# Building the stage-2 sine tables on all 128 lanes, loading K weights earlier and holding back the Wo copies

## The chip, the cores and the metric

The kernel runs on one core of one Trainium2 chip. The metric is microseconds (us) of device time for one execution. Executions of the kernel before alone spread from 2157.94 to 2175.35 us within one call of eleven runs, that is 0.8%. So a few us of change are hard to see in whole times, and much of this study reads *marks* in the traces: the moment at which a certain instruction ends or a certain store is issued.

## The reference

Two independent parts share the core, and their outputs stand side by side.

```python
def _A_ref(q, k, v, shift_k, ssm_k, ssm_D):       # S = 2048, D = 1024
    # k_shift: a causal convolution of k with 4 taps
    kv = k_shift * v
    # a long causal convolution by FFT of length 2 * S, per channel
    y = irfft(rfft(kv_padded) * rfft(ssm_k_padded))[:S]
    return q * (y + kv * ssm_D)

def _B_ref(x, mem0, Wq, Wk, Wv, Wo, seg_len):     # 32 heads of 128, 64 segments of 32
    mem = mem0
    for s in range(n_seg):
        h = concat([mem, x_segment])              # 8 memory rows and 32 new ones
        # q, k, v = h Wq, h Wk, h Wv; masked softmax attention; o = (...) Wo
        mem = o[:, :8]
        outs.append(o[:, 8:])
```

The kernel does part A's FFT by matrix products in a front of about 440 us. In the same time it computes the K and Q projections of all x for part B (those need no memory). Then come 64 segments, one after the other, which stream weights from DRAM.

## The kernel before

The front first makes the tables Mre, Mim, Nre, Nim of the second FFT stage by sines. VectorE computes integer phases, and ScalarE evaluates the sine of one lane block after another, because each block of lanes goes to other columns of the table:

```python
def act_sin(out_ap, a_int_ap, nbits, p0=0):
    nc.scalar.activation(out_ap, a_int_ap, ACT.Sin, bias=pi_col[p0:...], scale=...)
...
for x, (M, n) in enumerate(((Mre, nxr), (Mim, nxi))):
    aM = phases(x)...                              # VectorE: phases
    for (r0, c0) in [(0, 0), (64, 32)]:
        act_sin(M[r0:r0 + 64, :, c0:c0 + 32], aM[r0:r0 + 64], 12, r0)
for y, (N, ph) in enumerate(((Nre, (1024, 0)), (Nim, (2048, 1024)))):
    ...
    for (r0, c0) in [(0, 0), (32, 64), (64, 0), (96, 64)]:
        act_sin(N[r0:r0 + 32, :, c0:c0 + 64], aN[r0:r0 + 32], 12, r0)
```

Then stage 1 runs over 16 rows. A few words first: a lane is one of the 128 rows of a tile; an eviction is the copy of a finished matmul result (`s_ps`) to a tile from which it can be stored (`s_sb`); a chunk is a piece of weights of 512 KB; a unit is one step of stage 2. A row has two halves: the k half (transposes, a copy to `kt`, four matmuls, two evictions by ScalarE, one store to SK) and the u half (eight products on VectorE, four matmuls, two evictions by ScalarE, one store to SU):

```python
for t in range(16):
    # 8 transposes of ssm_k on the tensor engine
    nc.scalar.copy(kt[:], pt[:])
    stage1(kt, t, SK1)             # matmuls, 2 ScalarE evictions s_sb, store
    ...                            # loads of k and v, every second row
    # uacc and prod: 7 VectorE products and sums
    nc.vector.tensor_tensor(out=u[:], in0=acc[:], in1=Vt, op=ALU.mult)
    su_stores.append(stage1(u, t, SU1))
stage1_done(su_stores)
```

`stage1_done` belongs to part B. It loads x rows, transposes them to XBT (copied by ScalarE), loads eight K-weight chunks `pw`, each held until the store of a certain row has been issued, and runs the first K projection, 128 matmuls into `kb_ps`:

```python
make_xbt(su)                       # x loads held to su[X_LOAD + tb]
for kc in range(8):
    with tc.issue_after(su[K_LOAD + kc].ins):
        group(0, 0, which=[kc], ws=ws)
for _ in dense(0, 0, ws): pass     # kb_ps
```

Stage 2 of the FFT follows in units of `pa`, `pb` products. Between units `fill()` does some of part B's work. Every third unit it transposes one block of x; a load `X_sb` fetches two blocks at a time and is asked for when both blocks before it are done. It also issues the copies of Wo chunks from DRAM to the ring buffer in DRAM:

```python
if n >= WO_COPY and wo_copies:
    nc.gpsimd.dma_start(dst_view(stream_src(ch), ch), dram_chunk(ch))
if n % 3 == 2 and blocks:
    b = blocks.pop(0)
    x_block(b)
    if b % 2 and blocks:
        x_load(b + 1)
```

A scheduler decides the final order of the instructions on each engine, its queue.

Of the kernel before, what the change touches and what calls it, by code (L numbers as in the profile page):

```python
# [24 lines left out]
INLINE = {1: 0, 3: 1, 5: 0, 11: 1, 12: 0, 14: 1}  # L25
N2, N3 = 12, 15
WO_COPY = 27
X_LOAD, K_LOAD = 3, 7
RING = 6

PITCH = 2048


def a_kernel(ctx: ExitStack, tc, q, k, v, shift_k, ssm_k, ssm_D, outa, slot16, stage1_done, fill):
    nc = tc.nc
    S, D = 2048, 1024
    NP = 34
    NS = 17
# [10 lines left out]
    Mre = const.tile([128, NP, 64], BF, name="Mre")  # L49
    Mim = const.tile([128, NP, 64], BF, name="Mim")  # L50
    Nre = const.tile([128, NS, 128], BF, name="Nre")
    Nim = const.tile([128, NS, 128], BF, name="Nim")
# [4 lines left out]
    with ExitStack() as c1:  # L57
# [15 lines left out]
        def phases(x):  # L73
            return ints[:, 1088 * (x + 1):1088 * (x + 2)]
# [33 lines left out]
        def act_sin(out_ap, a_int_ap, nbits, p0=0):  # L108
            nc.scalar.activation(out_ap, a_int_ap, ACT.Sin, bias=pi_col[p0:p0 + out_ap.shape[0], 0:1],
                                 scale=-2.0 * PI / (1 << nbits))  # L110
# [57 lines left out]
        for hf in range(4):  # L168
            pt = ps_big.tile([128, 1024], F32, tag="big", name="sh_ps")
            for e in range(2):  # L170
# [18 lines left out]
        nxr = cw.tile([128, 1], F32, name="nxr")  # L189
        nc.vector.tensor_tensor(out=nxr[:], in0=nx[:], in1=phr[:], op=ALU.add)  # L190
        nxi = cw.tile([128, 1], F32, name="nxi")
# [5 lines left out]
        nc.vector.tensor_scalar(out=w_f[:], in0=w_i[:], scalar1=kp[:, 0:1], scalar2=None, op0=ALU.add)  # L197
        nc.vector.tensor_tensor(out=aN0, in0=w_f[:].unsqueeze(2).to_broadcast([128, NS, 32]),
                                in1=kn2[:].unsqueeze(1).to_broadcast([128, NS, 32]), op=ALU.mult)
        for x, (M, n) in enumerate(((Mre, nxr), (Mim, nxi))):  # L200
            aM = phases(x).rearrange("p (a b) -> p a b", b=32)
            nc.vector.tensor_scalar(out=aM, in0=v_i, scalar1=p_n2[:, 0:1], scalar2=n[:, 0:1], op0=ALU.mult, op1=ALU.add)
            nc.vector.tensor_scalar(out=aM, in0=aM, scalar1=4095, scalar2=None, op0=ALU.bitwise_and)
            for (r0, c0) in [(0, 0), (64, 32)]:
                act_sin(M[r0:r0 + 64, :, c0:c0 + 32], aM[r0:r0 + 64], 12, r0)
            nc.gpsimd.memset(M[32:64, 0, :], 0.0)
        for y, (N, ph) in enumerate(((Nre, (1024, 0)), (Nim, (2048, 1024)))):
            aN = phases(y).rearrange("p (a b) -> p a b", b=64)
            for x in range(2):
                nc.vector.tensor_scalar(out=aN[:, :, 32 * x:32 * x + 32], in0=aN0, scalar1=ph[x], scalar2=None, op0=ALU.add)  # L210
            nc.vector.tensor_scalar(out=aN, in0=aN, scalar1=4095, scalar2=None, op0=ALU.bitwise_and)
            for (r0, c0) in [(0, 0), (32, 64), (64, 0), (96, 64)]:
                act_sin(N[r0:r0 + 32, :, c0:c0 + 64], aN[r0:r0 + 32], 12, r0)

        def stage1(u_tile, t, scratch):
            sb = wk.tile([128, 2, 1024], BF, tag="s1_sb", name="s1_sb")
            for h in range(2):
                pt = ps_big.tile([128, 1024], F32, tag="big", name="s1_ps")
                for hf in range(2):
                    nc.tensor.matmul(pt[:, hf * 512:(hf + 1) * 512], lhsT=F1h[h][:, :],  # L220
                                     rhs=u_tile[:, hf * 512:(hf + 1) * 512], start=True, stop=True)
                nc.scalar.copy(sb[:, h, :], pt[:])
            return nc.sync.dma_start(scratch.rearrange("m (r h) d -> r m h d", h=2)[t], sb[:])
# [8 lines left out]
        for t in range(16):  # L232
            pt = ps_t.tile([128, 1024], BF, tag="ktp", name="k_tp")
            for db in range(8):
                src = KS[:, db, :].rearrange("p (n r) -> p r n", r=16)[:, t, :]
                nc.tensor.transpose(pt[:, db * 128:(db + 1) * 128], src, ident[:])
            kt = wk.tile([128, 1024], BF, tag="kt", bufs=2, name="kt")
            nc.scalar.copy(kt[:], pt[:])
            if t == 0:
                nc.vector.tensor_tensor(out=kt[0:1, :], in0=kt[0:1, :], in1=Drow[0:1, :], op=ALU.add)  # L240
            stage1(kt, t, SK1)
            if t % 2 == 0:
                K0 = k0pool.tile([128, 2048], BF, tag="K0", name="K0")
                nc.sync.dma_start(K0[:], pair_rows(k, t))
                ktiles[t], ktiles[t + 1] = K0[:, 0:1024], K0[:, 1024:2048]
                Vp = io.tile([128, 2048], BF, tag="Vt", name="Vt")
                nc.gpsimd.dma_start(Vp[:], pair_rows(v, t))
            Vt = Vp[:, 1024 * (t % 2):1024 * (t % 2) + 1024]
            acc = wk.tile([128, 1024], BF, tag="uacc", bufs=2, name="uacc")
            for li, lag in enumerate((3, 2, 1, 0)):  # L250
                Kl = ktiles[t - lag]
                if li == 0:
                    nc.vector.tensor_tensor(out=acc[:], in0=Kl, in1=SH[:, lag, :], op=ALU.mult)
                else:
                    pr = wk.tile([128, 1024], BF, tag="prod", bufs=2, name="prod")
                    nc.vector.tensor_tensor(out=pr[:], in0=Kl, in1=SH[:, lag, :], op=ALU.mult)
                    nc.vector.tensor_tensor(out=acc[:], in0=acc[:], in1=pr[:], op=ALU.add)
            u = wk.tile([128, 1024], BF, tag="u", bufs=2, name="u")
            nc.vector.tensor_tensor(out=u[:], in0=acc[:], in1=Vt, op=ALU.mult)
            su_stores.append(stage1(u, t, SU1))  # L260

    stage1_done(su_stores)

# [126 lines left out]
def b_kernel(ctx: ExitStack, tc, x, mem0, Wq, Wk, Wv, Wo, outb, n_seg, run_a):  # L390
    nc = tc.nc
# [35 lines left out]
    def dram_chunk(ch):  # L427
        m, a, g = ch
        return Wo_v[a] if m == 3 else W_v[m][a, g]

    def dst_view(ap, ch):
        return ap.rearrange("p (hh d) -> p hh d", hh=2) if ch[0] == 3 else ap

    def stream_src(ch):
        return WS[ring_order.index(ch), :, 0:2048]
# [3 lines left out]
    REC = dram.tile([128, n_seg, 768], BF, name="REC")  # L439
# [125 lines left out]
    def x_block(b):  # L565
        X_sb = loaded.pop(b)
        if b % 2 == 0:
            t = base.tile([128, 2048], BF, tag="wring3", name="xt")
            xts[b], xts[b + 1] = t[:, 0:1024], t[:, 1024:2048]
        tp = ps0.tile([128, 1024], BF, tag="ps0", name="xt_ps")  # L570
        for kc in range(8):
            nc.tensor.transpose(tp[:, kc * 128:(kc + 1) * 128], X_sb[:, kc * 128:(kc + 1) * 128], ident[:])
        xt = xts.pop(b).rearrange("p (s k t) -> p s k t", s=4, k=8)
        nc.vector.tensor_copy(xt, tp[:].rearrange("p (k j t) -> p j k t", k=8, j=4))
        nc.gpsimd.dma_start(REC[:, 4 * b:4 * b + 4, 0:256], xt.rearrange("p s k t -> p s (k t)"))

    xts = {}
    flip = [0]

    def evac(dst, src):  # L580
# [48 lines left out]
    def fill():  # L629
        store()  # L630
        n = units[0]
        units[0] += 1
        if n == 0:
            x_load(0)
        if n >= WO_COPY and wo_copies:
            ch = wo_copies.pop(0)
            nc.gpsimd.dma_start(dst_view(stream_src(ch), ch), dram_chunk(ch))
        if n % 3 == 2 and blocks:
            b = blocks.pop(0)
            x_block(b)  # L640
            if b % 2 and blocks:
                x_load(b + 1)
        if n >= 34 or n % 3 != 2:
            next(rest, None)

    run_a(slot16, stage1_done, fill)

    wres3 = ctx.enter_context(tc.tile_pool(name="b_wres", bufs=1, reuse_waits="tile"))
    for i, ch in enumerate(parts[1]):
# [169 lines left out]
    with tc.manual_schedule():  # L819
# [53 lines left out]
        for s in range(n_seg):  # L873
            b, j = s // NB, s % NB
# [188 lines left out]
@with_exitstack  # L1063
def kernel(
    ctx: ExitStack,
    tc: tile.TileContext,
    A_q: bass.AP,
    A_k: bass.AP,
    A_v: bass.AP,
    A_shift_k: bass.AP,  # L1070
    A_ssm_k: bass.AP,
    A_ssm_D: bass.AP,
    B_x: bass.AP,
    B_mem0: bass.AP,
    B_Wq: bass.AP,
    B_Wk: bass.AP,
    B_Wv: bass.AP,
    B_Wo: bass.AP,
    B_seg_len,
    out: bass.AP,  # L1080
):
    assert int(B_seg_len) == 32
    S = B_x.shape[1]
    n_seg = S // 32
    outa = out[0, :, 0:1024]
    outb = out[0, :, 1024:2048]
    def run_a(slot16, stage1_done, fill):
        with ExitStack() as ctx_a:
            a_kernel(ctx_a, tc, A_q[0], A_k[0], A_v[0], A_shift_k, A_ssm_k, A_ssm_D, outa, slot16, stage1_done, fill)

    with ExitStack() as ctx_b:
        b_kernel(ctx_b, tc, B_x[0], B_mem0[0],
                 B_Wq.rearrange("d h e -> d (h e)"), B_Wk.rearrange("d h e -> d (h e)"),
                 B_Wv.rearrange("d h e -> d (h e)"), B_Wo.rearrange("h e d -> (h e) d"),
                 outb, n_seg, run_a)
# [35 lines left out]
```

## Time and profile before

| Stretch of the trace before | What is there | us |
|---|---|---|
| to about 15 | constants, first loads | 15 |
| 15 to 115.3 | stage 1 with the sine tables; the last product ends at 104.7, the last row store is issued at 115.28 | 100 |
| 119 to 151.0 | first K projection | 32 |
| 152 to 359.8 | stages 2 and 3, to the last store of part A's output tile `ot` | 208 |
| to 465.95 | preparation of the segments, first segment output stored | 106 |
| to 2169.1 | 64 segments, to the last output store | 1703 |

The median was 2167.91 us when the prediction was made. The views that the prediction quotes carry the first three rows. In the timeline that it quotes, brackets hold the idle time before and what ended it. In the timeline of the kernel before (start, duration, engine, line; in brackets the idle time before and what ended it) the seventh unit of stage 2 looks like this:

```profile
172.58 0.38 SPq L561 DMA_DIRECT2D X_sb<-in_B_x_dram  x1
...
184.01 1.03 PE L572 MATMUL xt_ps<-ident,X_sb 128*128 128x128 bf16 x8 [3.50 <-DMA X_sb<-in_B_x_dram]
...
188.29 0.69 DVE L327 TENSOR_TENSOR pa<-Ure_ps,Kre 128x512 bf16<-128x512 f32 x1 [5.52 <-PE Ure_ps L307]
```

The second load of x is issued at 172.58 and the transposes that need it begin at 184.01. VectorE waits 5.5 us for the matmuls that stand behind those transposes.

### The profile page before, as it was taken

Reading aid. Unit: us, or ns where it says so; the run is one execution under the profiler, and the core shown is the slowest. Engines: PE = TensorE matmul, PEld = TensorE weight load, DVE = VectorE, ACT = ScalarE, POOL = GpSimd, SP = SyncE. Lnnn points to the kernel's source line nnn. Section 1 sums busy time; section 2 is a strip of 40 time slices with the busy share of each in tenths; the row PEclk is TensorE's granted clock in tenths of the full one; section 3 lists DMA queues with packets and bytes.
Section 4 is the critical chain, followed back from the end, with each engine's and each line's share of the span. In section 5 each row is a group of like instructions: output and inputs, shape, how many; then the busy total and the mean of one; then the engine's idle time right before and its main releaser. Section 6 shows DMA issues by size and latency. Waiting matters only on the chain. (4 is left out here: it accounts for less than half of the span.)

```text
span 2178.7 us, 81250 instructions
## 1 busy us (share of the span) xinstructions
PE 1731.8 (79%) x35605; PEld 927.3 (43%) x35636; DVE 872.5 (40%) x2691; ACT 649.2 (30%) x1139; POOL 426.2 (20%) x1100
## 2 busy tenths in 40 slices
PE   4688988978778787888878888888877887887776
PEld 2232333434444444444444444444444444444444
DVE  9826762133333333333333333333333333333332
ACT  7845531222222222222222222222222222222221
POOL 3013422301111111212111111111111111111111
PEclk9888999989999999999999999999999999999999
DMA  8999869999999999999999999999999999999996
GB/s 313 338 345 320 288 244 382 312 373 396 393 367 387 391 369 386 391 390 386 392 380 387 386 389 389 395 384 387 388 386 379 374 377 385 380 391 386 379 380 264
DMA packets 238311, 802.29 MB, mean 368 GB/s; under 512 B 34721, under 2 KB 34753, under 8 KB 237953
## 3 DMA queue, kind: packets, MB, share of 16 engines
q1 hardware_dynamic: 207186, 728.20, 87.6%
q0 software_dynamic: 25552, 58.39, 7.9%
q10 hardware_dynamic: 5216, 10.49, 1.3%
q8 instruction: 279, 4.57, 0.9%
q14 instruction: 78, 0.64, 0.1%
HBM read 737.56 MB, written 62.39 MB: 367 GB/s over the span
## 5 line engine op out<-in xcount | busy, mean ns | idle before, releaser
L907 PEld LDWEIGHTS <-rec 128*32 128x32 bf16 x12351 | 321.3, 96 | 481.5 <-issue 258.6
L907 PE MATMUL acc<-wring,rec 128*32 128x512 bf16 x3765 | 373.8, 386 | 146.5 <-DMA wring<-WS 130.5
L916 ACT CAST qkv_sb<-acc 128x512 bf16<-128x512 f32 x384 | 225.1, 586 | 664.0 <-PE acc L907 664.0
L993 PEld LDWEIGHTS <-OT 128*32 128x32 bf16 x8192 | 218.3, 97 | 177.7 <-issue 149.4
L993 PE MATMUL yacc<-wring,OT 128*32 128x256 bf16 x3072 | 155.9, 279 | 93.9 <-DMA wring<-WS 51.0
L907 PE MATMUL acc<-Wmid,rec 128*32 128x512 bf16 x3072 | 225.9, 384 | 0.0
L907 PE MATMUL acc<-Wres,rec 128*32 128x512 bf16 x2816 | 223.1, 382 | 0.0
L853 PEld LDWEIGHTS <-OTB 128*16 128x16 bf16 x4096 | 105.0, 90 | 106.2 <-issue 95.3
L979 ACT CAST OT<-OTp 128x512 bf16<-128x512 f32 x128 | 75.0, 586 | 241.9 <-PE OTp L971 241.7
L1009 DVE COPY KT<-tps 128x512 bf16<-128x512 bf16 x64 | 27.2, 425 | 297.1 <-PE tps L922 297.1
L980 DVE CAST OTB<-OTp 128x128 bf16<-128x128 f32 x128 | 37.3, 292 | 261.7 <-ACT OT L979 261.7
L808 POOL DMA_DIRECT2D rec<-REC x64 | 37.5, 586 | 528.4 <-issue 259.0
L755 DVE TENSOR_SCALAR wring<-OTp 128x384 int32<-128x384 int32 x126 | 112.3, 891 | 57.0 <-PE acc L907 47.7
L907 PE MATMUL acc<-pw,rec 128*32 128x512 bf16 x1544 | 132.5, 386 | 0.0
L883 POOL COPY KT<-rec 128x128 bf16<-128x128 bf16 x128 | 38.8, 303 | 426.7 <-PE SB L931 426.7
L937 DVE TENSOR_REDUCE mx<-SB 128x5 f32<-128x200 f32 x128 | 47.1, 368 | 186.9 <-PE SB L931 186.9
L868 POOL DMA_DIRECT2D out_dram<-YB x128 | 73.3, 579 | 241.5 <-DVE YB L866 220.1
L853 PE MATMUL SB<-wring,OTB 128*16 128x256 bf16 x1488 | 78.7, 275 | 40.8 <-DVE SB L832 32.8
L922 PEld LDWEIGHTS <-qkv_sb 128*128 128x128 bf16 x1024 | 63.0, 98 | 106.6 <-ACT qkv_sb L916 64.0
L922 PE MATMUL tps<-ident,qkv_sb 128*128 128x128 bf16 x1024 | 101.6, 222 | 8.2 <-ACT qkv_sb L916 0.3
L993 PE MATMUL yacc<-Wlate,OT 128*32 128x256 bf16 x2048 | 106.2, 277 | 2.4 <-issue 1.6
L1049 ACT CAST Y<-yacc 128x256 bf16<-128x256 f32 x64 | 23.8, 373 | 245.6 <-PE yacc L993 241.7
(231 smaller groups left out, 2657.7 us busy)
## 6 DMA issues: line engine op xcount, KB each, us to landing
wring<-WS SPq DMA_DIRECT2D x1215, 512.0 KB, 7.4
rec<-REC POOLq DMA_DIRECT2D x64, 192.0 KB, 6.0
SK<-s_sb SPq DMA_DIRECT2D x16, 512.0 KB, 4.5
SU<-s_sb SPq DMA_DIRECT2D x16, 512.0 KB, 4.6
Kg<-SK SPq DMA_DIRECT2D x32, 256.0 KB, 5.5
Ug<-SU SPq DMA_DIRECT2D x32, 256.0 KB, 5.9
REC<-stage POOLq DMA_DIRECT2D x16, 512.0 KB, 11.2
zt<-SZ SPq DMA_DIRECT2D x16, 512.0 KB, 7.7
```

Source lines behind the costliest of these rows:

```text
L755: nc.vector.tensor_scalar(out=dst, in0=src, scalar1=0, scalar2=None, op0=ALU.bitwise_or)
L808: nc.gpsimd.dma_start(rec[:], REC[:, s, :])
L853: nc.tensor.matmul(self.acc[32 * dq:32 * dq + W, x - o:y - o], lhsT=self.OTB[:, c, 4 * g + i, :], rhs=r, start=first and not self.seeded, ...
L868: nc.gpsimd.dma_start(bass.AP(outb.tensor, outb.offset + (SEG * NB * self.b + NX) * 2048 + 256 * dq, [[2048 * SEG, NB], [2048, 8], [1, 256 ...
L883: nc.gpsimd.tensor_copy(KT[:, :, :, 32:40], KBs[:, 128 * g:128 * g + 128].rearrange("p (c i t) -> p i c t", c=4, i=4))
L907: nc.tensor.matmul(self.acc[32 * c:32 * c + 32, x - 512 * c:y - 512 * c], lhsT=hT[:, kc, :], rhs=r, start=(kc == 0 and x == 512 * c), stop ...
L916: nc.scalar.copy(sb[:], self.acc[:])
L922: nc.tensor.transpose(tp[:, i * 128:(i + 1) * 128], sb[:, i * 128:(i + 1) * 128], ident[:])
L937: nc.vector.tensor_reduce(out=mx[:], in_=S, op=ALU.max, axis=AX.X)
L979: nc.scalar.copy(OT[:], o_view[:, :, :, 0:32])
L980: nc.vector.tensor_copy(OTB[:, :, 4 * g:4 * g + 4, 8 * j:8 * j + 8], o_view[:, :, :, 32:40])
L993: nc.tensor.matmul(yacc[32 * dq:32 * dq + 32, x - o:y - o], lhsT=OT[:, c, i, :], rhs=r, start=(h == 0 and x == o), stop=(h == 31), tile_po ...
```

## The change

Its intent: ScalarE evaluates each table with one sine on all 128 lanes into a scratch tile, 4 sines instead of 12, and VectorE copies the lane blocks to their places. The four tables are made between the first four rows and not before them. K chunks may be loaded beside rows 0 to 7 and not only after rows 7 to 15. Copies of Wo wait for the latest store of transposed x, so that the scheduler cannot move them into stage 1.

```diff
-X_LOAD, K_LOAD = 3, 7
+X_LOAD, K_LOAD = 4, 0
...
+            sines = slot4()[:, 0:32 * NP].rearrange("p (a b) -> p a b", b=32)
+            act_sin(sines, aM, 12)
             for (r0, c0) in [(0, 0), (64, 32)]:
-                act_sin(M[r0:r0 + 64, :, c0:c0 + 32], aM[r0:r0 + 64], 12, r0)
+                nc.vector.tensor_copy(M[r0:r0 + 64, :, c0:c0 + 32], sines[r0:r0 + 64])
...
+            sines = slot4()[:, 0:64 * NS].rearrange("p (a b) -> p a b", b=64)
+            act_sin(sines, aN, 12)
             for (r0, c0) in [(0, 0), (32, 64), (64, 0), (96, 64)]:
-                act_sin(N[r0:r0 + 32, :, c0:c0 + 64], aN[r0:r0 + 32], 12, r0)
+                nc.vector.tensor_copy(N[r0:r0 + 32, :, c0:c0 + 64], sines[r0:r0 + 32])
...
             su_stores.append(stage1(u, t, SU1))
+            if tables:
+                tables.pop(0)()
...
-            nc.gpsimd.dma_start(dst_view(stream_src(ch), ch), dram_chunk(ch))
+            with tc.issue_after(rec_stores[-1].ins):
+                nc.gpsimd.dma_start(dst_view(stream_src(ch), ch), dram_chunk(ch))
```

(The loops become functions `table_m` and `table_n`, `rec_stores` collects the stores of transposed x, and `slot4` is handed through.)

More of the change, by code (lines that the diff above doesn't have):

```diff
@@ L27, with a_kernel @@
 WO_COPY = 27
-X_LOAD, K_LOAD = 3, 7
+X_LOAD, K_LOAD = 4, 0
 RING = 6
 PITCH = 2048
-def a_kernel(ctx: ExitStack, tc, q, k, v, shift_k, ssm_k, ssm_D, outa, slot16, stage1_done, fill):
+def a_kernel(ctx: ExitStack, tc, q, k, v, shift_k, ssm_k, ssm_D, outa, slot4, slot16, stage1_done, fill):
     nc = tc.nc
@@ L199, in a_kernel, with table_m @@
                                 in1=kn2[:].unsqueeze(1).to_broadcast([128, NS, 32]), op=ALU.mult)
-        for x, (M, n) in enumerate(((Mre, nxr), (Mim, nxi))):
+        def table_m(x, M, n):
             aM = phases(x).rearrange("p (a b) -> p a b", b=32)
@@ L203, in a_kernel, with table_n @@
             nc.vector.tensor_scalar(out=aM, in0=aM, scalar1=4095, scalar2=None, op0=ALU.bitwise_and)
+            sines = slot4()[:, 0:32 * NP].rearrange("p (a b) -> p a b", b=32)
+            act_sin(sines, aM, 12)
             for (r0, c0) in [(0, 0), (64, 32)]:
-                act_sin(M[r0:r0 + 64, :, c0:c0 + 32], aM[r0:r0 + 64], 12, r0)
+                nc.vector.tensor_copy(M[r0:r0 + 64, :, c0:c0 + 32], sines[r0:r0 + 64])
             nc.gpsimd.memset(M[32:64, 0, :], 0.0)
-        for y, (N, ph) in enumerate(((Nre, (1024, 0)), (Nim, (2048, 1024)))):
+        def table_n(y, N, ph):
             aN = phases(y).rearrange("p (a b) -> p a b", b=64)
@@ L211, in a_kernel @@
             nc.vector.tensor_scalar(out=aN, in0=aN, scalar1=4095, scalar2=None, op0=ALU.bitwise_and)
+            sines = slot4()[:, 0:64 * NS].rearrange("p (a b) -> p a b", b=64)
+            act_sin(sines, aN, 12)
             for (r0, c0) in [(0, 0), (32, 64), (64, 0), (96, 64)]:
-                act_sin(N[r0:r0 + 32, :, c0:c0 + 64], aN[r0:r0 + 32], 12, r0)
+                nc.vector.tensor_copy(N[r0:r0 + 32, :, c0:c0 + 64], sines[r0:r0 + 32])
+        tables = [lambda: table_m(0, Mre, nxr), lambda: table_m(1, Mim, nxi),
+                  lambda: table_n(0, Nre, (1024, 0)), lambda: table_n(1, Nim, (2048, 1024))]
         def stage1(u_tile, t, scratch):
@@ L574, in x_block @@
         nc.vector.tensor_copy(xt, tp[:].rearrange("p (k j t) -> p j k t", k=8, j=4))
-        nc.gpsimd.dma_start(REC[:, 4 * b:4 * b + 4, 0:256], xt.rearrange("p s k t -> p s (k t)"))
+        rec_stores.append(nc.gpsimd.dma_start(REC[:, 4 * b:4 * b + 4, 0:256], xt.rearrange("p s k t -> p s (k t)")))
     xts = {}
+    rec_stores = []
     flip = [0]
@@ L644, in fill @@
             next(rest, None)
-    run_a(slot16, stage1_done, fill)
+    run_a(pair, slot16, stage1_done, fill)
     wres3 = ctx.enter_context(tc.tile_pool(name="b_wres", bufs=1, reuse_waits="tile"))
@@ L1086, with run_a @@
     outb = out[0, :, 1024:2048]
-    def run_a(slot16, stage1_done, fill):
+    def run_a(slot4, slot16, stage1_done, fill):
         with ExitStack() as ctx_a:
-            a_kernel(ctx_a, tc, A_q[0], A_k[0], A_v[0], A_shift_k, A_ssm_k, A_ssm_D, outa, slot16, stage1_done, fill)
+            a_kernel(ctx_a, tc, A_q[0], A_k[0], A_v[0], A_shift_k, A_ssm_k, A_ssm_D, outa, slot4, slot16, stage1_done, fill)
     with ExitStack() as ctx_b:
```

## The prediction

> **What bounds the kernel now.** I read the page of the kernel before first, for the shape of the run. It has a front (convolution and weight loading) of about 440 us, then 64 like segments.
>
> ```profile
> DVE  9826762133333333333333333333333333333332
> ACT  7845531222222222222222222222222222222221
> DMA  8999869999999999999999999999999999999996
> GB/s 313 338 345 320 288 244 382 312 373 396 393 367 387 391 369 386 391 390 386 392 380 387 386 389 389 395 384 387 388 386 379 374 377 385 380 391 386 379 380 264
> ```
>
> A slice is 54 us. From slice 9 on the DMA engines are always in tenth nine: the segments stream weights and the change does not touch them. It touches the first two slices (VectorE and ScalarE both nearly full) and, by moving copies, slices 5 and 6. Second, the busy times by stretch (PE, PEld, DVE, ACT, POOL, clock, DMA share, GB/s):
>
> ```profile
> 20.00:40.00 20.00, 6.02 (x22) 2.46 (x23) 19.96 (x34) 19.75 (x19) 6.66 (x12) 1.00 0.92 321
> 80.00:100.00 20.00, 12.28 (x62) 5.39 (x62) 17.65 (x30) 17.47 (x20) 1.61 (x3) 0.91 0.99 367
> 100.00:119.00 19.00, 11.68 (x40) 4.53 (x41) 6.05 (x22) 17.69 (x23) 0.81 (x3) 0.62 0.97 337
> 119.00:127.00 8.00, 6.02 (x19) 1.86 (x19) 0.00 (x0) 1.32 (x3) 0.56 (x1) 0.84 0.99 347
> 275.00:300.00 25.00, 22.80 (x114) 7.90 (x116) 18.05 (x32) 13.39 (x25) 8.77 (x9) 1.00 0.45 146
> ```
>
> Through the 16 rows of stage 1 VectorE and ScalarE are both saturated; after 104.7 us, where the last row's product ends, VectorE is idle and ScalarE alone is behind. Then 119 to 127 us belongs to nobody: the tensor engine waits. Third, the timeline of that place (start, us, engine, line):
>
> ```profile
> 22.00 4.83 ACT L109 ACTIVATE Nre<-ints,pi_col 32x1088 bf16<-32x1088 int32 x4
> 26.85 4.83 ACT L109 ACTIVATE Nim<-ints,pi_col 32x1088 bf16<-32x1088 int32 x4
> 31.71 1.93 ACT L222 CAST s_sb<-s_ps 128x1024 bf16<-128x1024 f32 x2
> ...
> 104.01 0.69 DVE L259 TENSOR_TENSOR u<-uacc,Vt 128x1024 bf16<-128x1024 bf16 x1
> ...
> 115.14 4.25 ACT L537 COPY XBT<-xbt_ps 128x512 bf16<-128x512 bf16 x8
> 115.65 1.73 SPq L551 DMA_DIRECT2D pw<-in_B_Wk_dram  x3
> 118.95 3.37 PE L594 MATMUL kb_ps<-XBT,pw 128*128 128x512 bf16 x9 [0.67 <-ACT XBT L537]
> 123.00 0.82 PE L594 MATMUL kb_ps<-XBT,pw 128*128 128x512 bf16 x3 [0.68 <-DMA pw<-in_B_Wk_dram]
> 125.64 0.60 PE L594 MATMUL kb_ps<-XBT,pw 128*128 128x512 bf16 x2 [0.71 <-DMA pw<-in_B_Wk_dram]
> 126.70 5.56 PE L594 MATMUL kb_ps<-XBT,pw 128*128 128x512 bf16 x24
> ```
>
> The sines hold ScalarE from 17.1 to 31.7 us, so its first row eviction comes at 31.7 and it never catches up: the last one ends at 115.2, 10.5 us behind VectorE. Eight XBT copies follow, and the K projection (128 matmuls at L594) then waits for three K-weight chunks that are issued only at 115.65. It runs freely from 126.7 to 151.0: 111 matmuls in 24.3 us, 0.219 each. Only then does stage 2 start.
>
> **What the Trainium skill says.** "ScalarE: Activation LUTs", section "What ACT_TABLE_LOAD costs", puts an ACTIVATE with a pointer bias at 280 ns plus 0.833 ns per element of a lane, whatever the lanes: 1186 ns for 1088 elements. The trace agrees: 1199 ns on 32 lanes, 1199 to 1200 on 64. "VectorE: DVE Perf Modes", section "The perf-mode tier table", puts a bf16 copy within SBUF at four elements a cycle (693 ns for 2048) and a tensor_tensor at two. The one such copy in the trace, 128x768 at L761, took 350 ns, which fits; the 1024-wide products take 680 ns. The same page, section "Two Vector instructions with no wait between them", says that an instruction whose output starts in another quadrant than the last one's is held until earlier ones finish; no instruction of the trace before shows it, and I use it only to count the copies in full length. "DMA: Bandwidth & Descriptors", section "Issuing engines are not separate DMA queues", says that transfers of all queues share the same 16 engines. That fits 318 to 367 GB/s at a share of 0.9 to 1.0 here, whoever issues.
>
> **The change part by part.** *Sines.* Removed: 12 ACTIVATEs (4 of 64 lanes, 8 of 32) at 1.2 us, 14.5 us. Added: 4 of 128 lanes and the same width, 4.8 us. ScalarE gets back 9.7 us, and in the built order it does the two evictions of the first k row before any sine; the two N tables come between rows. *Copies.* VectorE gains 12 copies of 1088 bf16 elements (4 on 64 lanes, 8 on 32). From the 350 ns copy: 768 elements at four per 0.96 GHz cycle are 200 ns, so 150 ns is fixed, and 1088 elements make 283 + 150 = 433 ns. Twelve are 5.2 us (an estimate; 4.2 if they overlap by 80 ns as the products do, started 602 ns apart for 680 ns).
>
> *Stage 1 after.* The first M sine now ends near 21.0 us (k eviction, then sine), and VectorE's first copy and row start there, 21.1 us. From there: 128 products of 0.602 are 77.1 us; the N phases, four adds and two masks, about 3.8; copies 5.2 or less. The last product ends at 21.1 + 77.1 + 3.8 + 5 = 107 us, later than the 104.7 of before. ScalarE's own sum from 21 us is 62 evictions and 14 kt copies at 0.93, the sines and 4.2 us of XBT copies, about 79 us, so it is done by 100 and keeps 7 us of slack. The tail behind the last product is then two matmuls (0.9) and two evictions (1.9): the last one ends near 110, against 115.2.
>
> *K weights.* In the built order of the SP queue all eight K chunks stand before the stores of the last three rows, and seven of eight XBT copies lie among the rows. On the tensor engine the 128 L594 matmuls follow the last row at once. So both gaps, 115.2 to 118.95 and the slow running to 126.7, go. The projection starts at 110 to 111 and takes 128 x 0.219 = 28 us: end at 138.5 instead of 151.0, so 12.5 us earlier. The Wmid weights for the next step (12 x 0.52 MB) and the stage-2 gathers, about 8.9 MB from 111 us on at 345 GB/s, need until 137: just in time.
>
> *Wo copies.* Six DRAM-to-DRAM copies of 0.52 MB (8.6 us of DMA at 365 GB/s) leave 22.5 to 27 us and come, by the built POOL order, after fill 27, near 255 to 275 us of the new timeline. The stretch 275 to 300 has 55% of 25 us idle DMA, 13.7 us, so they fit. But they stand on the POOL queue between transposed-x stores, and a VectorE copy of such a tile has waited 6.3 us for its store at 263 already. I charge 3 us.
>
> *Sum.* -12.5 + 3 = -9.5 us. VectorE bounds stage 2 nearly (22.9 of 25 us busy from 200 to 225), the tensor engine 360 to 420 us (59.7 of 60), so an earlier start passes through to the segments: 2167.9 - 9.5 = 2158.4, say 2159.
>
> **Rivals.** *A: VectorE takes the gain.* It was full already and gets 5 us more. If the copies ran at one element per cycle (1088 / 0.96 + 150 = 1.28 us each, 15 us in all), the last product would come at 117 and stage 1 would end later than now; only the weights' gap would be won, some 5 us: 2163. The contiguous 32- or 64-element runs and the L761 copy speak against it. *B: DMA takes the gain.* From 21 to 110 us the changed kernel must move 32 row stores, K, V, x, eight K chunks and four WS copies, about 30.8 MB, 346 GB/s, against 337 to 367 seen at a share of 0.97 to 0.99. Evictions would wait for row stores (before: 6.3 us of waits on SK and SU) and the end of stage 1 slips to 113 to 115: total 2162 to 2165. What speaks against it is that 3.1 MB of Wo copies leave this stage and that ScalarE has slack to absorb waits. *C: the held copies collide.* If stage 2's or 3's gathers queue behind them in full, 8.6 us come back: 2164. *D: it all fits*, and the Wo copies vanish in the hole: 2155.
>
> **Range and chances.** A and B together have some weight, C a little, and the three timed runs before spread over 5 us. The range 2150 to 2166 holds the main case, D and most of A to C. Two per cent is 43 us, nearly the whole 46 us between the last product and stage 2's start, of which 28 are matmuls that stay: faster 0.01, same 0.98, slower 0.01.
>
> **What would show it.** Right: four ACTIVATEs of 128x1088 near 1.2 us; twelve copies near 0.43 us; VectorE's last product near 107 and ScalarE's last row eviction some 3 us behind it; L594's block unbroken from about 110 to 138.5 with no wait on K weights; Wo copies near 255 to 275 where the share is below one; segments the same, 9 to 10 us earlier. Wrong: copies over 0.8 us (A); longer landings of row stores and evictions waiting for them, or L594 waiting for a chunk (B); waits on x stores or gathers in the last third of stage 2, so that the lead shrinks between 138 and 300 us (C).

## The result, and the profile after

The changed kernel took 2162.12 us in the median of four runs (2160.3 to 2168.5), against 2168.97 us (2166.85 to 2172.2, four runs) for the kernel before. The ratio is 0.9972 with a 95% interval of 0.9948 to 0.9997. A ratio is the mean time of one kernel's runs over that of the other's of the same rounds, so it is not quite the ratio of the medians quoted. The class is "within 2%". The two profiled runs differ by 18.5 us in span (2178.7 and 2160.2), but only 6.4 us of that arises before the first segment's output. Nearly all the rest is in the segment loop, whose code did not change: from first to last output store it took 1703.2 us before and 1690.4 after, and 1684.9 to 1693.2 in the first four experiments. I take that part for variation between runs, since the one kernel that was traced twice already differs by 3.5 us there (1690.4 and 1686.9). So spans of single profiles must not be compared here.

The busy rows of the page after, and then the busy times by stretch (PE, PEld, DVE, ACT, POOL, clock, DMA share, GB/s), for four of the stretches that the prediction shows of before:

```profile
DVE  9937752133333333333333333333333333333332
ACT  6845521222222222222222222222222222222221
DMA  8999989899999999999999999999999999999996
```

```profile
20.00:40.00 20.00, 8.03 (x32) 3.20 (x33) 18.61 (x32) 13.39 (x15) 3.19 (x7) 0.73 0.69 224
100.00:119.00 19.00, 11.20 (x37) 3.99 (x37) 11.49 (x31) 17.14 (x22) 0.78 (x3) 0.79 0.92 342
119.00:127.00 8.00, 7.85 (x31) 3.30 (x31) 0.69 (x1) 3.57 (x6) 0.00 (x0) 0.85 0.81 289
275.00:300.00 25.00, 21.16 (x97) 8.17 (x99) 14.30 (x26) 8.66 (x17) 6.93 (x7) 0.93 0.76 268
```

Four readings. ScalarE is far less busy between 20 and 40 us (13.39 against 19.75), yet in 100 to 119 it is as busy as before (17.14 against 17.69): it still ends stage 1 in arrears. VectorE's work now reaches further into 100 to 119 (11.49 against 6.05). The DMA engines are much freer in 20 to 40 (share 0.69 against 0.92) and busier in 275 to 300 (0.76 against 0.45, after Wo copies that were issued at 261 to 274). The gap of the tensor engine at 119 to 127 us is closed (7.85 busy of 8, against 6.02). The timeline of the kernel after shows how stage 1 begins and ends:

```profile
19.95 2.30 ACT L109 ACTIVATE pair<-ints,pi_col 128x1088 bf16<-128x1088 int32 x2
29.44 1.93 ACT L230 CAST s_sb<-s_ps 128x1024 bf16<-128x1024 f32 x2 [6.29 <-remote]
41.29 2.88 DVE L218 COPY Nre<-pair 32x1088 bf16<-32x1088 bf16 x4
59.30 1.93 ACT L230 CAST s_sb<-s_ps 128x1024 bf16<-128x1024 f32 x2 [3.98 <-issue]
...
110.39 0.69 DVE L267 TENSOR_TENSOR u<-uacc,Vt 128x1024 bf16<-128x1024 bf16 x1 [0.96 <-PE s_ps L228]
118.95 1.96 ACT L230 CAST s_sb<-s_ps 128x1024 bf16<-128x1024 f32 x2
119.45 28.93 PE L605 MATMUL kb_ps<-XBT,pw 128*128 128x512 bf16 x125
120.94 0.32 SPq L231 DMA_DIRECT2D SU<-s_sb  x1
261.08 2.04 POOL L649 DMA_DIRECT2D WS<-in_B_Wo_dram  x3
```

The sines are short, but what ScalarE wins it spends waiting: 6.3 us at 29.4 for the matmuls of VectorE's first `u`, 4 us at 59.3 for those of the fifth, and 2.6 us for phases (next view). (The profile names no engine for the first two; the matmuls of these `u` begin just before, at 28.4 and 58.2.) The last product ends at 111.1, the last row eviction at 120.9. The K projection starts only at 119.45, but then it runs to 148.4 in one piece, without a wait for weights. What ScalarE waited for between 15 and 118 us (us in total, times, longest), as the view of waits lists it:

```profile
ACT s_sb L230 <- remote: 6.3, 1, 6.3
ACT s_sb L230 <- DMA SU<-s_sb: 5.1, 4, 2.1
ACT s_sb L230 <- issue: 4.0, 1, 4.0
ACT s_sb L230 <- PE s_ps L228: 2.9, 4, 1.8
ACT pair L109 <- DVE ints L214: 2.6, 1, 2.6
```

In that stretch of 103 us ScalarE (the fourth busy time of these rows, before and then after) was busy 91.89 us before and 79.36 after, so its idle time rose from 11.1 to 23.6 us:

```profile
15.00:118.00 103.00, 57.43 (x267) 26.72 (x272) 87.02 (x154) 91.89 (x98) 11.87 (x23) 0.85 0.94 327
15.00:118.00 103.00, 58.66 (x265) 26.24 (x270) 94.04 (x166) 79.36 (x88) 7.69 (x17) 0.78 0.88 309
```

The waits for row stores (SU and SK together) are about what they were, 6.5 us against 6.3. The groups of the copies (count, busy us, mean ns, idle before); the four sines have a mean of 1218 ns in the same view:

```profile
L218 DVE COPY Nre<-pair 32x1088 bf16<-32x1088 bf16 x4 | 2.8, 709 | 0.0
L207 DVE COPY Mre<-pair 64x1088 bf16<-64x1088 bf16 x2 | 0.9, 438 | 2.2 <-ACT pair L109 2.1
```

Where the lead arises, from the same marks in both traces (the right column is the changed kernel run once more, c1 below):

| Mark | before | after | lead | lead, second trace |
|---|---|---|---|---|
| last row store of stage 1 issued | 115.28 | 120.94 | -5.7 | -5.8 |
| K projection ends | 151.03 | 148.38 | 2.6 | 2.5 |
| seventh unit of stage 2 starts | 188.29 | 179.81 | 8.5 | 6.2 |
| last `ot` store issued | 359.76 | 351.83 | 7.9 | 6.8 |
| first segment output stored | 465.95 | 459.56 | 6.4 | 6.5 |

Stage 1 became longer, the projection won that back and 2.6 us more, and the first units of stage 2 won as much again or more.

### The profile page after: what moved, and what is told of

Same layout as the page of the kernel before. It is cut to its first block, busy times and chain, and to the rows that moved or that the text cites. A ratio compares the mean times of both kernels' runs of the same rounds, so it can differ in the third digit from the quotient of the medians. Undisturbed runs are those within 1.5% of the kernel's fastest.

```text
span 2160.2 us, 81253 instructions
## 1 busy us (share of the span) xinstructions
PE 1727.5 (80%) x35605; PEld 930.2 (43%) x35636; DVE 878.7 (41%) x2703; ACT 638.1 (30%) x1131; POOL 424.5 (20%) x1100
## 5 line engine op out<-in xcount | busy, mean ns | idle before, releaser
L919 PEld LDWEIGHTS <-rec 128*32 128x32 bf16 x12351 | 324.1, 96 | 465.4 <-issue 248.9
L865 PEld LDWEIGHTS <-OTB 128*16 128x16 bf16 x4096 | 105.6, 90 | 104.7 <-issue 93.8
```

The lines of the kernel that those rows point to most:

```text
L865: nc.tensor.matmul(self.acc[32 * dq:32 * dq + W, x - o:y - o], lhsT=self.OTB[:, c, 4 * g + i, :], rhs=r, start=first and not self.seeded, ...
L919: nc.tensor.matmul(self.acc[32 * c:32 * c + 32, x - 512 * c:y - 512 * c], lhsT=hT[:, kc, :], rhs=r, start=(kc == 0 and x == 512 * c), stop ...
```

## The experiments

Twelve runs followed. Names: *S* is the sine part (with its X_LOAD of 4), *K* the early K weights (K_LOAD 0), *W* the held Wo copies. The letters of theories in the expectations are not those of the prediction's rivals. All gave correct results. The marks of all of them:

| Run | last product | last row store | projection ends | last `ot` store | first output | ratio to before, 95% interval |
|---|---|---|---|---|---|---|
| before | 104.7 | 115.3 | 151.0 | 359.8 | 466.0 | 1 |
| after (S K W) | 111.1 | 120.9 | 148.4 | 351.8 | 459.6 | 0.9972 [0.9948, 0.9997] |
| a1: W | 102.0 | 112.3 | 147.4 | 352.4 | 459.2 | 0.9991 [0.9965, 1.0017] |
| a2: K | 105.1 | 115.4 | 149.6 | 358.8 | 465.4 | 1.0001 [0.9975, 1.0028] |
| a3: S | 110.8 | 121.6 | 157.3 | 365.5 | 473.3 | 1.0016 [0.9988, 1.0043] |
| a4: S K | 112.5 | 122.6 | 150.1 | 352.9 | 459.9 | 0.9992 [0.9970, 1.0014] |
| b1: S W | 111.3 | 123.2 | 157.5 | 360.6 | 468.8 | 1.0036 [1.0009, 1.0063] |
| b2: K W | 106.2 | 116.9 | 150.1 | 359.4 | 466.8 | 0.9982 [0.9948, 1.0016] |
| b3: after, even copies | 110.6 | 121.1 | 148.5 | 352.2 | 462.5 | 0.9964 [0.9941, 0.9988] |
| b4: after, k rows ahead | 110.0 | 119.7 | 140.8 | 347.9 | 456.4 | 0.9974 [0.9953, 0.9994] |
| c1: after again | 111.0 | 121.0 | 148.5 | 353.0 | 459.5 | 0.9984 [0.9955, 1.0013] |
| c2: even copies and k rows ahead | 107.1 | 116.5 | 137.6 | 346.8 | 455.8 | 0.9964 [0.9932, 0.9996] |
| c3: before, split x loads | 104.2 | 114.7 | 149.9 | 356.0 | 464.9 | 0.9997 [0.9967, 1.0028] |
| c4: c2 with split x loads | 107.7 | 118.3 | 139.4 | 345.0 | 451.2 | 0.9945 [0.9908, 0.9982] |

How well a mark repeats, c1 tells: 0.1 us in stage 1, 2.3 us at the seventh unit of stage 2, 1.1 us at the last `ot` store, 0.1 us at the first output. Two other pairs give a warning: c2 and c4 differ only in later code, and yet their last row stores lie 1.8 us apart; b3 agrees with the changed kernel within 0.5 us at four marks, and yet its first output comes 2.9 us later. A difference below about 3 us in a single trace shows nothing for certain. The timed ratios agree in direction for the larger ones only.

### a1: only the Wo copies held

```diff
+            with tc.issue_after(rec_stores[-1].ins):
                 nc.gpsimd.dma_start(dst_view(stream_src(ch), ch), dram_chunk(ch))
```

> The kernel before with one part of the change alone: the six Wo copies held behind the transposed-x stores (fill 27 on). Marks used in all runs: issue of the last row store of stage 1 (before 115.3 us, changed kernel 120.9), first Y store of the segments (before 466.0, changed 459.6). Theory D (the gain is the 3.1 MB of Wo copies leaving the opening, which the DMA engines fill up to about 190 us): the first Y store comes at 458 to 462, ratio about 0.997, without any help of sines or weights. Theory W (the gain is the K weights' wait that goes) and theory S (the gain is the 9.7 us of sines): nothing changes, first Y store 465 to 467, ratio 1.000.

The last row store came 3.0 us earlier and the last `ot` store 7.4 us earlier: theory D's mark was met, and at the last `ot` store and the first output (459.2 against 459.6) this line alone has about the whole lead of the changed kernel. Evictions waited 3.5 us for row stores, against 6.3 before. That stage 1 gains when six copies leave it fits its DMA share (0.86 against 0.94 between 15 and 118 us). Late in stage 2 the copies cost nothing that the marks show. Why the lead grows from 3.0 us at the end of stage 1 to 7.4 at the last `ot` store is not shown. The timed ratio (0.9991) cannot confirm 7 us; its interval reaches from 0.9965 to 1.0017.

### a2: only the K weights early

```diff
-X_LOAD, K_LOAD = 3, 7
+X_LOAD, K_LOAD = 3, 0
```

> The kernel before with K_LOAD 0 alone, so that the K weights come beside rows 0 to 7 and the Wo copies stay at 23 us. Theory W: the projection runs unbroken behind the rows, ends at 145 or earlier instead of 151, first Y store 459 to 461, ratio 0.997. Theory D: the same bytes have to pass by 190 us, so what the projection wins is given back in the following gathers: first Y store 464 to 466, ratio 0.999 to 1.000. S: as D.

Almost nothing moved: 1.4 us at the end of the projection, 1.0 us at the last `ot` store. The permission to load early is not the same as an early load: in the built order two K chunks still stand behind the last row store, and the projection again paused for them (a piece of 16 matmuls from 119.08, the next at 125.28). So theory W was not put to the test here.

### a3: only the sines

```diff
 # the changed kernel with
-X_LOAD, K_LOAD = 4, 0
+X_LOAD, K_LOAD = 4, 7
 # and without
-            with tc.issue_after(rec_stores[-1].ins):
```

> The kernel before with the sines on 128 lanes, the block copies and the interleaving alone (X loads from row 4, as the shared buffers ask). Theory S: ScalarE's last eviction comes several us before 115, first Y store at 457 to 461. Theory D, and what the trace of the changed kernel suggests (VectorE gains about 7 us of copies, ScalarE waits for phases between rows): the last row store is issued at 117 to 122, later than before, and the first Y store at 466 to 470, ratio 1.000 to 1.002.

The main part of the change, taken alone, loses: the last row store comes 6.3 us later and the projection ends 6.3 us later. Theory S fell; the first output, at 473.3, is even later than the 466 to 470 of theory D. The projection waits for K chunks, as the timeline of this run shows; it runs freely only from 130.99.

```profile
127.66 0.60 PE L605 MATMUL kb_ps<-XBT,pw 128*128 128x512 bf16 x2 [2.58 <-DMA pw<-in_B_Wk_dram]
```

### a4: everything but the held Wo copies

```diff
 # the changed kernel without
-            with tc.issue_after(rec_stores[-1].ins):
```

> The changed kernel with the Wo copies let free again (they go out in the first 30 us). Theory D: the lead over the kernel before is lost: first Y store 464 to 467, ratio 0.999 to 1.001. Theories W and S: it is kept, first Y store 459 to 461, ratio 0.997.

With the K weights early, the sines no longer lose: the projection runs in one piece from about 121 and ends at 150.1, 7.2 us before that of a3, and the last `ot` store lies 12.5 us before that of a3. K_LOAD 0 is worth 1.0 us without the sines and 12.5 us with them. The queues show a reason: here all eight K chunks are issued by 105.8 us (104.4 in the changed kernel), while in a2 the last two come at 115.8 and 116.3, behind the last row store. So the same edit gives early weights only beside the sine part, which also has X_LOAD 4; which of the two does it was not tested. Against the full change, holding the Wo copies is now worth only 1.1 us (0.0 against the second trace of the full change), where it was worth 7.4 us alone. Theory D, which a1 had borne out, would have had the lead lost. The parts do not add.

### b1 and b2: the two other pairs

b1 is the changed kernel with K_LOAD set back, b2 is the kernel before with the held copies and K_LOAD 0.

```diff
 # b1, on the changed kernel
-X_LOAD, K_LOAD = 4, 0
+X_LOAD, K_LOAD = 4, 7
```

> The changed kernel with K_LOAD back at 7 (sines and held Wo copies stay). What the first four runs left: sines alone set the first Y store 7.3 us later (473.3), K loads early alone 0.6 earlier, but both together 6.0 earlier. Theory I (the early weights are needed because the sines lengthen stage 1: without them the projection again waits for its last chunks, and the stage-2 loads take the other order): projection ends at 152 to 155, first Y store 466 to 470. Theory D (Wo copies alone carry the gain): 459 to 462.

```diff
 # b2, on the kernel before
-X_LOAD, K_LOAD = 3, 7
+X_LOAD, K_LOAD = 3, 0
+            with tc.issue_after(rec_stores[-1].ins):
                 nc.gpsimd.dma_start(dst_view(stream_src(ch), ch), dram_chunk(ch))
```

> The changed kernel without its sine part: before plus held Wo copies plus K_LOAD 0. If the sine part is a loss that the other two pay for, this is as fast as the whole change or faster: last row store near 112 as in the run with the Wo copies alone, first Y store 456 to 459. If the sine part is needed, the first Y store is at 460 or later.

b1 confirms a3: sines without early weights end the projection at 157.5 (theory I had said 152 to 155), and the timed ratio of 1.0036 [1.0009, 1.0063] is the only one whose interval lies wholly above 1. Its distance to the full change at the last `ot` store, 8.8 us (7.6 against its second trace), is the second measurement of what early weights are worth beside the sines. b2 is a surprise: held copies and early weights without the sines keep nothing of a1's 7.4 us (0.3 us at the last `ot` store). Its stage 1 ends 4.6 us later than a1's, and the seventh unit of stage 2 starts 36.0 us after the first, as in before. The cause is not shown. What the trace has: the evictions waited 8.1 us for row stores (3.5 in a1), and two K chunks were issued at 117.3 and 117.8, behind the last row store, as in a2. By its expectation b2 says that the sine part is needed; it may instead be the order of the K loads that comes with it, and no run separates the two.

### b3: the N copies in even halves

The N copies took 709 ns where I had worked out 433, while the M copies took 435 to 438. In the built program, as the trace records the operands, the source of an N copy is one run of 1088 elements per lane and the destination is 17 runs of 64. For an M copy it is 1088 and 34 runs of 32. b3 writes the same N copy as 2 x 17 x 32 on both sides.

```diff
-                nc.vector.tensor_copy(N[r0:r0 + 32, :, c0:c0 + 64], sines[r0:r0 + 32])
+                nc.vector.tensor_copy(N[r0:r0 + 32, :, c0:c0 + 64].rearrange("p a (h b) -> p h a b", h=2),
+                                      sines[r0:r0 + 32].rearrange("p a (h b) -> p h a b", h=2))
```

> The changed kernel with the eight N copies written as 2 x 17 x 32 instead of 17 x 64, the same bytes. In the changed kernel they took 709 ns each against 435 ns of the M copies (34 x 32) of the same size. Theory E (an odd outermost count halves the rate): 435 ns each, VectorE saves 2.2 us, last product at 108.9 instead of 111.1. Rival (32 lanes or their offset are slower): 709 ns as before. First Y store 0 to 2 us earlier than 459.6.

The group of these copies in b3:

```profile
L218 DVE COPY Nre<-pair 32x1088 bf16<-32x1088 bf16 x4 | 1.7, 433 | 0.0
```

So the odd outer count halves the rate: at two elements per cycle the working of the prediction gives 1088 / 2 / 0.96 GHz + 150 = 717 ns (an estimate), at four 433, and both were measured within 2%. This is what the Trainium skill says in "VectorE: DVE Perf Modes", section "What auto-detection actually checks": the mode of four elements a cycle needs the outermost dimensions of source and destination to be "both even or equal", and 1088 and 17 are neither. The rival of the expectation, that 32 lanes or their offset are slow, fell, since these stayed. I had used that page for the rate and not applied its condition. VectorE saved 8 x 0.276 = 2.2 us, but the last product ended only 0.4 us earlier, and the last row store not at all: the last two products now waited 1.0 and 1.5 us for matmuls that still read the `u` tile (1.0 us in all in the changed kernel), and those stood behind ScalarE's evictions. In the changed kernel VectorE's time is not what ends stage 1.

### b4: k rows two ahead

If ScalarE lacks work early because it waits for VectorE's first `u`, it should have other work in its queue there: the k halves need nothing of VectorE. b4 emits the k half of row t + 2 before the u half of row t.

```diff
-        for t in range(16):
+        def k_row(t):
             ...                      # transposes, kt, stage1(kt, t, SK1)
+        for t in range(2):
+            k_row(t)
+        for t in range(16):
+            if t + 2 < 16:
+                k_row(t + 2)
             ...                      # the u half, as before
```

> The changed kernel with the k rows (transpose, copy, stage 1 of k) emitted two rows ahead of the u rows, nothing else. Theory A (ScalarE idles some 20 us in the first rows and is two rows behind at the end, because k evictions stand behind u evictions in its order): it fills the early idle time, the last row store is issued at 112 to 116 instead of 120.9, projection ends 140 to 144, first Y store 452 to 456. Rival V (VectorE, or the row stores on the DMA engines, set the end): last row store at 119 or later, first Y store within 1 us of 459.6.

Neither theory fits whole. The last row store came only 1.2 us earlier (119.7, where theory A had said 112 to 116), and ScalarE, rid of the wait at 29.4, still idled 18.2 us between 21 us and its last row eviction (21.8 in the changed kernel). But the projection now starts at 107.96 beside the last rows, and ends at 140.8, 7.6 us earlier than in the changed kernel. The last `ot` store gains 3.9 us of that. So what held the projection in the changed kernel was its place in the tensor engine's queue, behind the last row's matmuls, which waited for ScalarE's arrears. Part of the 7.6 us is lost again in stage 2, whose seventh unit starts 36.0 us after the first instead of 30.3: there the tensor engine waited for x again, 6.0 us.

### c1: the changed kernel once more

> The changed kernel itself once more, to see how well the marks of one trace repeat. If the marks carry the argument, the last product ends at 111 +- 1 us, the last row store is issued at 121 +- 1, the last store of the transposed outputs of stage 2 and 3 (ot) at 352 +- 2, the first Y store at 460 +- 3, and the ratio to the kernel before is 0.996 to 0.998. If the front differences of 1 to 7 us that I read between variants are noise, the ot mark moves by more than 3 us from 351.8.

The marks repeat, as said above the experiments. The timed ratio, 0.9984, lies just outside the expected 0.996 to 0.998, and its interval includes 1: taken alone, this does not show a gain. And one thing did not repeat. I had come to believe that the change removes the stall at the seventh unit, because the first trace of the changed kernel has hardly a wait there (0.6 us on the tensor engine's weight loads). The same kernel, with the same order on every queue, shows it in its second trace:

```profile
178.28 0.62 PE L582 MATMUL xt_ps<-ident,X_sb 128*128 128x128 bf16 x8 [4.68 <-DMA X_sb<-in_B_x_dram]
```

It costs less than before all the same: the seventh unit starts 32.5 us after the first, not 36.1. Of these 3.6 us 1.2 are won by the start of the sixth unit and 2.4 behind it; why is not shown. So the stall differs between executions of one program, and "the order of the load queue removed it" is not true as I had put it.

### c2: b3 and b4 together

> The changed kernel with both earlier edits: N copies in even halves and k rows two ahead. If the two add: last product near 109.5, last row store near 119, K projection over by 140, seventh stage-2 unit still 36 us after the first (it waits for the second x load), last ot store 347 to 348, first Y store 455 to 460, ratio 0.995 to 0.998. If stage 2 takes the lead away, ot is back at 352.

Together the last product ends at 107.1, 3 us before that of either alone, and the last row store is issued at 116.5. It looks as if VectorE's 2.2 us count once ScalarE is supplied, though stage 1 of c4, with the same code, was 0.6 us slower at the last product and 1.8 us at the last row store. At the last `ot` store this makes 346.8, 1.1 us before b4 and so as far as a mark moves by itself.

### c3: the kernel before with x loads in halves

```diff
-            if b % 2 and blocks:
-                x_load(b + 1)
+            if b + 2 < n_seg // 4:
+                x_next(b + 2)         # one block, into the half of block b
```

> The kernel before with one edit: x for stage 2 is loaded in halves, so that the load of the third block is asked for one unit after the first block is free and not only when both are. Theory (the 5.5 us stall at the seventh unit is the late second x load, and the change removed it by the order of the load queue): seventh unit at 30 to 31 us after the first instead of 36.1, PE waits on X_sb from 3.5 us to under 1, last ot store at 354 +- 1.5 against 359.8, stage 1 as before (last product 104.7, last row store 115.3), ratio 0.997 to 0.999. Rival (the stall is DMA crowding at that place, and moves to the next transfer): the wait comes back at another unit, and ot stays at 358 to 360.

The wait on x is gone from the tensor engine (ScalarE shows one of 1.0 us), and the seventh unit starts 30.8 us after the first instead of 36.1:

```profile
178.97 0.61 PE L580 MATMUL xt_ps<-ident,X_sb 128*128 128x128 bf16 x8
```

The last `ot` store comes 3.8 us earlier than in before, not the 5.8 that I expected: the stall is real and can be removed by itself, and some two thirds of it reach the mark. At the first output 1.1 us are left, and the timed ratio shows nothing (0.9997).

### c4: all three edits on the changed kernel

c4 is b3, b4 and the split x loads together.

> The changed kernel with even N copies, k rows two ahead and x loads in halves: a candidate to beat both. If the stall at the seventh unit is won on top of the earlier projection: seventh unit 30 to 32 us after the first, last ot store 342 to 344, first Y store 450 to 455, ratio 0.993 to 0.995. If it is the same gain as the k rows give and can be had only once, ot stays at 347 to 348 and the ratio at 0.996 to 0.998.

The last `ot` store is issued at 345.0, one us later than the better theory said, and the first output is stored at 451.2, 14.7 us before that of before. The timed median was 2158.26 us, against 2164.97 for before and 2162.64 for the changed kernel; the ratio to before, 0.9945 [0.9908, 0.9982], is the best. Kernels are compared only within the same rounds. Against the changed kernel the mean ratio is 0.9967 (2156.0 over 2163.1 us), without an interval, and the single runs of the two overlap (2145.98 to 2163.12 and 2158.21 to 2168.79). That c4 beats before is shown. That it beats the changed kernel is shown at the marks and likely in time. In its timeline the projection starts while ScalarE still has rows to finish:

```profile
107.27 1.02 PE L620 MATMUL kb_ps<-XBT,pw 128*128 128x512 bf16 x4 [0.88 <-ACT XBT L554]
...
116.55 8.80 PE L620 MATMUL kb_ps<-XBT,pw 128*128 128x512 bf16 x40
118.31 0.32 SPq L232 DMA_DIRECT2D SU<-s_sb  x1
```

## Why the prediction was right, and which steps were not

The time was predicted as 2159 us in a range of 2150 to 2166, and 2162.12 was measured. The sum was -9.5 us; the medians give -6.9 and the first output stored 6.4. The total is right within the range, but its terms are not: several errors cancelled, and that was luck. Nor does the number choose between the cases, since 2162.12 lies nearer to the rivals A, B and C (2162 to 2165) than to the 2159 of the main case.

- **Sines.** Right. Four sines of 128 lanes took 1218 ns each, where 1.2 us was worked out.
- **Copies.** Right for M (435 to 438 ns), wrong for N. "Twelve are 5.2 us" was 4 x 0.437 + 8 x 0.709 = 7.4 us. The cause, the odd outer count, is shown by b3. Counting them in full length, after "VectorE: DVE Perf Modes", section "Two Vector instructions with no wait between them" (an instruction whose output starts in another group of 32 lanes than the last one's is held until the earlier ones have finished), was right, and the trace agrees: behind a copy that starts at lane 0 the next product starts after 0.35 us (of 0.43), behind one that starts at lane 64 only after 0.47, and four N copies to four such groups took 2.88 us for 4 x 0.709. The slow N copies are a small form of rival A, at half rate instead of a quarter; b3 shows also that it did not set the end of stage 1.
- **End of stage 1: the step that failed.** I wrote that ScalarE's work is done by 100 us, that it "keeps 7 us of slack", that the last product ends at 107 and the last eviction some 3 us behind it, near 110. The product ended at 111.1, where 2.2 us are the N copies and 1.0 a wait for the `u` tile, and the eviction at 120.9, 9.8 us behind it (10.5 before). ScalarE's own work was sized well (from 21 us to its last row eviction 79 us were worked out and 78.1 measured), but I took work and time for the same: in that stretch it also idled 21.8 us. It works through a fixed queue: it waited 6.3 us for the first `u`, 2.6 us for phases between rows and several more for matmuls that wait for `u`, and what stood further back came later too. Its idle time between 15 and 118 us doubled. With about 4.9 us of ScalarE work in a row (four evictions at 0.97 and a `kt` copy of 1.03) and 4.8 us on VectorE, it has no speed in hand to catch up. That the queue's order matters is shown by b4 and c2; which of the waits is decisive was not separated.
- **K weights.** The mechanism was right: no wait on a weight chunk is left in the first projection, and it runs in one piece. The size was off: -12.5 us was -2.6 at its end, since it started at 119.45 and not at 110. a3 and b1 show that without early weights the sines lose 6.3 and 6.4 us there.
- **Wo copies.** They come at 261 to 274 us, within the predicted 255 to 275. I charged 3 us, and no cost is to be seen. a1 shows a gain of 7.4 us instead, which the sum had not as a term: 3.0 us of it at the end of stage 1, which 3.1 MB of copies left, and the rest in later stages, by a way that is not shown. Within the full change this gain is hardly there (0 to 1.1 us from a4), so it may not be added.
- **Passing through.** "An earlier start passes through to the segments" held from the seventh unit on, but for about 2 us at most. What I had not foreseen is that the first seven units of stage 2 would win 3.6 to 5.9 us themselves, in a stretch where the DMA engines are full (share 1.01 before and 1.03 after between 150 and 190 us, 360 and 378 GB/s). That gain and the 3 us that the Wo copies did not cost make up for most of the 10 us that the projection fell short, and so the total came out near without the reasons being right.
- **Rivals.** B fell as put, though its total fits: waits for row stores did not grow (6.5 us against 6.3), and the late end of stage 1 has other causes. C fell: the lead does not shrink behind the copies by more than 1 us before the last `ot` store. D's point on the copies was right.

Still open: by which way the held copies alone gain 7.4 us (a1), why held copies and K_LOAD 0 together gain nothing without the sines (b2), and how much of the gain in stage 2 is the stall at the seventh unit. That stall varies from trace to trace of the same kernel; c3 shows that its removal alone is worth about 4 us at the last `ot` store.

## What to carry to other kernels

Time taken off an engine is a gain only if the engine's queue holds work that is ready at that moment; read the waits of the engine after the change, not only its sum of busy time, and look for independent work to emit further ahead. Parts of a change that share a bound do not add: test them alone and in pairs, as here one part lost alone and another was worth 1 us or 12.5 depending on the rest. Look in the built queue whether an edit did what it was meant to: the same constant brought all eight loads ahead of the last rows in one build and only six in another. When an unchanged loop of 1700 us varies by 18 us between traces, compare marks ahead of it and run the kernel twice before a mark is trusted.

## What the Trainium skill lacked or had wrong

- "VectorE: DVE Perf Modes", section "What auto-detection actually checks": the rule is right here (709 ns for 17 runs, 432 to 438 ns with even counts), but it does not say that a contiguous 17 x 64 operand of the kernel's code can be built as one dimension of 1088, so that source and destination, which look equal in the code, are not.
- No page that I drew on warns that time freed on an engine with a fixed queue can be lost to waits: ScalarE was 12.5 us less busy between 15 and 118 us, and stage 1 still ended 5.7 us later.
- No page that I drew on gives the spread of a kernel bound by DMA: 2157.94 to 2175.35 us over eleven runs of one kernel.
